# Pooled attention and a maxout FFN on one core: output stores cut by 128-token halves

## The chip, the cores and the metric

The kernel runs on one core of a Trainium2 chip. The metric is device time in microseconds. Before the change it is 230.5 us, the median of three runs (229.07 to 233.97). The profile is one more execution of the same program.

## The reference

Attention over keys and values that are averaged in groups of eight, for 8 batches of 8 heads, 576 positions and 64 dimensions a head; its output, with the heads side by side, is 4608 tokens of 512 features, and goes through an FFN whose hidden layer is the maximum of three products.

```
k_p = k.reshape(B, H, 72, 8, D).mean(axis=3);  v_p likewise
attn = softmax(q @ k_p.T / 8);  x = (attn @ v_p) -> [4608, 512]
h   = max(max(x @ w1, x @ w2), x @ w3)          # w1..w3: 512 x 768
out = h @ w_out                                 # 768 x 512, float32, [4608, 512]
```

## The kernel before

**Attention** runs batch by batch: scores on PE (tile `psf`), the exponent on ACT (`et`), the product with the values on PE (`pav`), the normalised result on DVE (`xn`). From batch 3 on the result is turned to features-by-tokens by a DMA transpose on SP's queue (`turn_x`, L256, into `xT`), and the queries of later batches likewise (L305, `qb` into `qT`). k, v and q come in by DMAs that are issued from POOL's queue and convert to 16 bits on the way.

**The FFN** takes tiles of 512 tokens, n = 0 to 8. h is w1's product plus the maximum of zero and two differences; the w1 part goes straight through a merged weight `wm`, the others through `hT`. Tiles 1 to 7 end in `out_product`: seven products per tile by a Strassen-like scheme, evacuated by ACT and DVE into an SBUF buffer `osb` of [128 partitions, 2 halves, 512 features]; a tile has two of them (j = 0 and 1), and three are in rotation. When the products of one buffer are all there, `store` writes it to DRAM. Tile 0 has its own stores in `project` (L421). Tile 8 ends in `out_last`, which runs each product for one half m of 128 tokens at a time and keeps its results in one buffer `ob`, [128, 2 (j), 2 (m), 512]; its stores are made by columns (`lo` and `hi`, 256 each) on three queues: j = 1 `hi` and j = 0 `hi` on SP, j = 1 `lo` on ACT, j = 0 `lo` on POOL.

**How tokens lie.** The kernel works on the 576 rows of a batch in nine groups of 64: group g holds the rows r * 9 + GS[g], r = 0 to 63, with GS = (0, 2, 4, 6, 8, 1, 3, 5, 7). A half m of an output buffer is two neighbouring groups: u = 0 on partitions 0 to 63 and u = 1 on 64 to 127. `store` before (L685 to L692) goes by u: the two halves m = 0 and 1 of one u are groups g and g + 2, and where GS[g + 2] = GS[g] + 4 within the batch, one DMA takes both, with the pattern 64 rows x 2 x columns in DRAM; else there are two DMAs of 64 rows each.

**Order.** The order of work on every engine is written out by hand (the string ORDER and the list for the last tile), and each queue issues in that order: on SP the stores stand between the transposes. In the built program each transfer on SP's queue also waits for the one that was issued eight transfers earlier to have landed, since eight completion semaphores are used in turn.

Of the kernel before, what the change touches and what calls it, by code (L numbers as in the profile page):

```python
# [14 lines left out]
def kernel(  # L15
# [11 lines left out]
    nc = tc.nc  # L27
# [3 lines left out]
    B, H, S, D = q.shape  # L31
# [10 lines left out]
    NG = 9  # L42
    GS = (0, 2, 4, 6, 8, 1, 3, 5, 7)
# [18 lines left out]
    def psum(shape, dtype, name, tag, bufs):  # L62
        return pools[-1].tile(shape, dtype, name=name, tag=tag, bufs=bufs)
# [5 lines left out]
    def matmul(*args, **kw):  # L69
        latest[0] = nc.tensor.matmul(*args, **kw)  # L70
        return latest[0]
# [66 lines left out]
    for sign in (1, -1):  # L138
        nc.gpsimd.affine_select(
            out=pick, in_=pick, compare_op=ALU.is_ge, fill=0.0, base=7 * (sign < 0),  # L140
            pattern=[[sign, 6], [-8 * sign, 128]], channel_multiplier=6 * sign)
    for i in range(3):
        load_w(slice(256 * i, 256 * i + 256))
    nc.gpsimd.dma_start(
        out=wo_sb, in_=moe_w_out.rearrange("(jc p) c -> p jc c", p=128))
# [378 lines left out]
    def take(key, shape=(128, 2, 256)):  # L524
        i = free_banks.pop(0)
        taken[key] = i, psum(list(shape), F32, name="pb", tag=f"pb{i}", bufs=1)
        return taken[key][1]

    def give(key):
        free_banks.append(taken.pop(key)[0])  # L530
# [80 lines left out]
    def of(i):  # L611
        return "B" if i == 2 else "C" if i in (4, 7) else "A"
# [69 lines left out]
            nc.vector.tensor_tensor(out=hTs[n][:, j, c], in0=relus[j], in1=b, op=ALU.max)  # L682
        give("n")

    def store(e, n, j, o, c):  # L685
        for u in range(2):
            b, g = divmod(2 * (4 * n + 2 * j) + u, NG)
            pair = g + 2 < NG and GS[g + 2] == GS[g] + 4
            for m in range(0, 2, 1 + pair):
                b, g = divmod(2 * (4 * n + 2 * j + m) + u, NG)  # L690
                dst = out[S * b:S * b + S, :].rearrange("(r g) c -> r g c", g=NG)
                e.dma_start(out=dst[:, GS[g]:GS[g] + 4 * pair + 1:4, c],  # L692
                            in_=o[64 * u:64 * u + 64, m:m + 1 + pair, c])

    def out_operands(n, i, m, r):
        za, zb = PRODUCTS[i]
        c = slice(128 * m, 128 * m + 128)
        if isinstance(zb, str):
            z = int(zb[1]) - 1
            left = xs[n % 2][:, z, r, c] if r < 2 else ths[n][:, z, r - 2, c]  # L700
        else:
            at = HALF * (zb % 2) + 128 * m
            left = (tokens(NB * n + at, NB * n + at + 128)[:, 2 * (zb // 2) + r] if r < 2
                    else hTs[n][:, JH * (zb // 2) + r - 2, at:at + 128])
        h, r = (0, r) if r < 2 else (1, r - 2)
        right = so[h][:, int(za[1]) - 1, r] if isinstance(za, str) else out_w(za, h)[:, r]
        return left, right

    outs = {}
    lo, hi = slice(0, HALF), slice(HALF, C)  # L710

    def out_product(n, i):
# [27 lines left out]
        if i in (5, 7, 3) and all((n, z, "d") in done for z in (5, 7, 3)):  # L740
            store(nc.sync, n, 1, o(1), slice(0, C))
        if i in (2, 4) and all((n, z, "d") in done for z in (2, 4)):
            store(nc.sync, n, 0, o(0), slice(0, C))

    def out_last(n):

        o = sb2.tile([128, 2304], F32, name="ob", tag="et")[:, 0:2048].rearrange(
            "p (j m c) -> p j m c", j=2, m=2)
        banks, ended = {}, set()

        def product(i, m):
            f = of(i)
            if (f, m) not in banks:
                banks[f, m] = (psum([128, HALF], F32, name="oC", tag=SC[0], bufs=SC[1])
                               if f == "C" else take((f, m), (128, HALF)))
            p = banks[f, m]
            for r in range(5):
                matmul(p, *out_operands(n, i, m, r), stop=(r == 4),
                                 start=(i in FIRST and r == 0), skip_group_check=True)
            ended.add((i, m))  # L760

            def plus(j, c):
                nc.vector.tensor_tensor(out=o[:, j, m, c], in0=o[:, j, m, c],  # L763
                                        in1=banks["B" if c == lo else "C", m], op=ALU.add)

            def both_of(*parts):
                return all((z, k) in ended for z in parts for k in range(2))

            if i in (1, 5, 6, 3):
                nc.scalar.copy(out=o[:, int(i in (5, 3)), m, lo if i in (1, 3) else hi],  # L770
                               in_=p)
            elif i == 2:
                plus(0, lo)
            elif i == 4:
                plus(0, hi)
            if i in (5, 7) and (12 - i, m) in ended:
                plus(1, hi)
            if i in (2, 3):
                give((f, m))
            if i in (5, 7) and both_of(5, 7):  # L780
                store(nc.sync, n, 1, o[:, 1], hi)
            if i == 3 and both_of(3):
                store(nc.scalar, n, 1, o[:, 1], lo)
            if i in (2, 4) and both_of(i):
                store((nc.gpsimd, nc.sync)[i // 4], n, 0, o[:, 0], (lo, hi)[i // 4])

        return product

# [149 lines left out]
```

## Time and profile before

| | |
|---|---|
| median of three runs | 230.5 us |
| profiled execution: time, span | 227.75 us, 225.9 us |
| mean granted clock of TensorE | 0.997 |
| L692 stores from `osb`, SP's queue | 43, issue 476 / 608 / 1189 ns (min / median / max) |
| L692 stores from `ob` | 4 on SP, 2 on POOL, 2 on ACT |
| landing of stores from `osb` after issue | 2.3 / 3.1 / 8.2 us |
| transposes on SP's queue | 27 for `xT`, 15 for `qT` |

The span is the time from the first to the last instruction in the profile; what the profiled execution took beyond it lies before and after. Landing is the time from the issue of a transfer to its completion semaphore. "SPq" and "ACTq" in the profile are the instruction streams of SP and ACT as they issue transfers.

### The profile page before, as it was taken

The page shows a single profiled execution, that of the slowest core. Times are in us where ns is not written, and L with a number is a line of the kernel's source. Part 1 is how long each engine was busy: PE and PEld are TensorE (multiplying, and loading weights), DVE is VectorE, ACT ScalarE, POOL GpSimd, SP SyncE. Part 2 cuts the span into 40 slices and gives each one's busy share as a digit, 9 for nine tenths or more (in the row PEclk, how much of TensorE's full clock was granted, in tenths as well). Part 3 has the DMA queues.
Part 4 walks back from the last instruction along what each step waited for, and adds up shares of the span by engine and source line. Part 5 has one row for each costly group of instructions (what it writes and reads, how often), then busy time and mean ns, then how long its engine had stood idle before and what let it go on. Part 6 is the DMA issues. An engine that isn't in the chain of part 4 may idle for free.

```text
span 225.9 us, 5235 instructions
## 1 busy us (share of the span) xinstructions
PE 212.3 (94%) x2046; PEld 165.7 (73%) x2046; DVE 180.2 (80%) x362; ACT 132.0 (58%) x264; POOL 82.7 (37%) x90
## 2 busy tenths in 40 slices
PE   7788999899999999998999996999999999999991
PEld 2377745558986666874679885988989898888881
DVE  3558967276999899987899965989989998988651
ACT  2267525687866887354369855957454571674230
POOL 7975300969419546459012027125140000000020
PEclk9999999999999999999999999999999999999998
DMA  6999999989999799989999999995371541430085
GB/s 166 208 197 197 204 207 205 204 160 236 151 156 132 126 163 182 151 171 194 134 211 172 155 125 171 195 156 107 70 166 36 136 105 31 115 73 0 4 229 141
DMA packets 50824, 33.57 MB, mean 149 GB/s; under 512 B 27280, under 2 KB 46352, under 8 KB 50800
## 3 DMA queue, kind: packets, MB, share of 16 engines
q0 software_dynamic: 20304, 16.98, 51.6%
q1 hardware_dynamic: 30208, 16.00, 40.8%
q8 instruction: 16, 0.26, 0.5%
q10 hardware_dynamic: 288, 0.26, 0.4%
q14 instruction: 8, 0.07, 0.1%
HBM read 34.60 MB, written 9.44 MB: 195 GB/s over the span
## 4 chain that ended last, share of the span: by engine, by line
PE 73%; DVE 11%; DMA 9%; issue 3%; ACT 1%; POOL 1%; SPq 0%; POOLq 0%; DVEq 0%; ACTq 0%
PE pb L70 54%; PE psf L70 5%; DMA qT<-qb 5%; PE pw L70 4%; PE pav L70 4%; DMA vt<-in_v_dram 4%; DVE xn L279 3%; PE pm L70 2%; PE pxt L74 1%; DVE hT L682 1%; DVE xs L537 1%; PE oC L70 1%; DVE kz L78 1%; DVE hs L537 1%; DVE rcp L277 1%
## 5 line engine op out<-in xcount | busy, mean ns | idle before, releaser
L70 PE MATMUL pb<-xT,mw 128*128 128x256 f16 (+1 forms) x312 | 52.8, 305 | 1.2 <-DVE hT L682 1.2
L70 PEld LDWEIGHTS <-mw 128*128 128x128 f16 x444 | 41.5, 98 | 16.3 <-issue 2.2
L807 POOL TENSOR_TENSOR half<-vt 72x512 f32<-72x512 f16 x28 | 32.9, 1189 | 52.9 <-DMA vt<-in_v_dram 42.6
L226 ACT ACTIVATE et<-psf 72x512 f16<-72x512 f32 x63 | 35.3, 595 | 8.2 <-PE psf L70 8.1
L279 DVE TENSOR_TENSOR xn<-pav,rcp 128x512 f16<-128x512 f32 x40 | 27.7, 691 | 1.4
L78 ACT COPY osb<-pb 128x512 f32<-128x512 f32 x25 | 14.7, 587 | 23.7 <-PE pb L70 23.7
L70 PE MATMUL psf<-qT,kz 128*128 128x256 bf16 (+4 forms) x161 | 21.3, 249 | 2.6 <-DMA qT<-qb 2.0
L636 DVE TENSOR_TENSOR ys<-ys,pb 128x512 f16<-128x512 f16 x30 | 20.3, 682 | 2.3 <-PE pb L70 2.0
L70 PEld LDWEIGHTS <-kz 128*128 128x128 bf16 x185 | 14.6, 98 | 8.5 <-issue 3.4
L70 PEld LDWEIGHTS <-hs 128*128 128x128 f16 x192 | 18.8, 98 | 2.2
L811 POOL TENSOR_TENSOR vt<-half 72x512 f16<-72x512 f32 x14 | 18.0, 1300 | 5.9 <-DVE xs L537 3.4
L692 POOL DMA_DIRECT2D out_dram<-ob x2 | 1.3, 636 | 50.1 <-DVE ob L763 50.1
L70 PE MATMUL pb<-mwo,hT 128*128 128x256 f16 (+1 forms) x120 | 19.3, 294 | 0.0
L70 PE MATMUL pb<-soh,hs 128*128 128x256 f16 x138 | 19.1, 273 | 0.0
L70 PEld LDWEIGHTS <-hT 128*128 128x128 f16 x168 | 16.3, 98 | 3.6
L78 ACT COPY pb<-pb 128x512 f32<-128x512 f32 x21 | 12.0, 575 | 10.8 <-PE pb L70 7.0
L70 PE MATMUL pav<-vp,et 72*128 72x65 f16 x320 | 17.1, 194 | 0.8 <-DVE xn L279 0.4
L78 ACT CAST ys<-pb 128x512 f16<-128x512 f32 x27 | 15.6, 593 | 3.6 <-PE pb L70 3.3
L70 PE MATMUL pb<-xs,sums 128*128 128x256 f16 x90 | 17.2, 272 | 0.1
L70 PEld LDWEIGHTS <-et 72*128 72x128 f16 x320 | 14.6, 98 | 3.5 <-DVE xn L279 1.4
L70 PE MATMUL pb<-xs,sw 128*128 128x256 f16 x90 | 17.2, 272 | 0.0
L645 ACT ACTIVATE t<-pb 128x256 f16<-128x256 f32 x30 | 11.2, 387 | 8.2 <-PE pb L70 7.8
(111 smaller groups left out, 413.0 us busy)
## 6 DMA issues: line engine op xcount, KB each, us to landing
out_dram<-osb SPq DMA_DIRECT2D x38, 128.0 KB, 2.7
ktFalse<-in_k_dram POOLq DMA_DIRECT2D x7, 576.0 KB, 13.2
qb<-in_q_dram POOLq DMA_DIRECT2D x7, 576.0 KB, 9.5
vt<-in_v_dram POOLq DMA_DIRECT2D x7, 576.0 KB, 14.1
out_dram<-osb SPq DMA_DIRECT2D x13, 256.0 KB, 3.7
mw<-in_moe_w_dram POOLq DMA_DIRECT2D x9, 256.0 KB, 9.5
ktTrue<-in_k_dram SPq DMA_DIRECT2D x3, 384.0 KB, 5.5
mwo<-in_moe_w_out_dram POOLq DMA_DIRECT2D x1, 768.0 KB, 13.3
```

What stands on the lines that cost most here:

```text
L70: latest[0] = nc.tensor.matmul(*args, **kw)
L74: latest[0] = nc.tensor.transpose(*args, **kw)
L78: (nc.vector.tensor_copy if on_vector[0] else nc.scalar.copy)(out=out, in_=in_)
L226: nc.scalar.activation(out=out, in_=in_, func=FT.Exp, scale=1.0 / 64.0)
L277: nc.vector.reciprocal(out=rcp, in_=pv[:, :, :, 64])
L279: nc.vector.tensor_tensor(out=xn, in0=pv[:, :, :, 0:D], in1=rcp.to_broadcast([128, 2, 4, D]), op=ALU.mult)
L537: t = e.tensor_tensor(out=out, in0=a, in1=b, op=op)
L636: nc.vector.tensor_tensor(out=y[:, j], in0=y[:, j], in1=bank("C", n, g), op=ALU.add)
L645: nc.scalar.activation(out=t0, in_=p[:, 0], func=FT.Relu)
L682: nc.vector.tensor_tensor(out=hTs[n][:, j, c], in0=relus[j], in1=b, op=ALU.max)
L807: yield e.tensor_tensor(out=f[:, c], in0=t[:, c, 0:4, :], in1=t[:, c, 4:8, :], op=ALU.add)
L811: yield e.tensor_tensor(out=t[:, c, 0:2, :], in0=f[:, c, 0:2, :], in1=f[:, c, 2:4, :], op=ALU.add)
```

## The change

`store` gets a list of halves, `parts`. Where both groups of a half lie two rows apart in one batch (GS[g + 1] = GS[g] + 2, that is for g other than 4 and 8) for all halves asked for, it issues one DMA per half: source the 128 partitions of that half, destination the pattern 2 groups x 64 rows x columns. Else it goes on as before. In `out_last` the last store (j = 0, `hi`) is issued for each half m as soon as that half's addition has been recorded, and no longer once for both.

```
-    def store(e, n, j, o, c):
+    def store(e, n, j, o, c, parts=(0, 1)):
+        whole = [m for m in parts if 2 * (4 * n + 2 * j + m) % NG not in (4, 8)]
+        if len(whole) == len(parts):
+            for m in parts:
+                b, g = divmod(2 * (4 * n + 2 * j + m), NG)
+                dst = out[S * b:S * b + S, :].rearrange("(r g) c -> r g c", g=NG)
+                e.dma_start(out=dst[:, GS[g]:GS[g] + 3:2, c].rearrange("r u c -> u r c"),
+                            in_=o[:, m, c])
+            return
         for u in range(2):
...
-            if i in (2, 4) and both_of(i):
-                store((nc.gpsimd, nc.sync)[i // 4], n, 0, o[:, 0], (lo, hi)[i // 4])
+            if i == 2 and both_of(2):
+                store(nc.gpsimd, n, 0, o[:, 0], lo)
+            if i == 4:
+                store(nc.sync, n, 0, o[:, 0], hi, (m,))
```

In the built programs nothing else differs on PE, ACT, DVE or POOL. SP issues 50 plain transfers in place of 58: from `osb`, 14 of 2x64x512 and 21 of the old forms in place of 43 of the old forms; from `ob`, 4 of 2x64x256 in place of 4 of 64x2x256. ACT's two stores and POOL's two have the new form 2x64x256 too. Of the transposes, those that follow the first new stores on SP's queue are the ones that the profile of before has from 101.78 us on.

## The prediction

> **What bounds the kernel now.** I read the page's slices first, then the chain that ended last, then the transfer views of single stages. The slices:
>
> ```profile
> span 225.9 us, 5235 instructions
> ...
> PE 212.3 (94%) x2046; PEld 165.7 (73%) x2046; DVE 180.2 (80%) x362; ACT 132.0 (58%) x264; POOL 82.7 (37%) x90
> ...
> DMA  6999999989999799989999999995371541430085
> ```
>
> PE is busy 94% of the span, so the kernel is PE-bound on average. But the DMA engines stand at nine tenths and over through slice 28, to about 158 us: until then whatever is put on an engine in addition comes out behind what is there. The chain between 95 and 200 us has one long piece that is no PE work:
>
> ```profile
> 126.84 0.32 SPq L256
> 127.16 0.05 issue
> 127.21 0.02 SPq L305
> 127.22 0.03 issue
> 127.25 10.34 DMA qT<-qb
> 137.59 0.04 issue
> 137.64 0.60 PE psf L70 x5
> ```
>
> A transpose by DMA, issued on SP's queue like the stores, lands at 137.59 us and PE uses it 0.05 us later. Issue and landing events give the same for its neighbours: the qT transposes issued at 103.51 and 108.13 land 2.7 and 1.6 us ahead of their first use, those issued at 143.98 and 145.37 0.9 and 1.5 us ahead. SP's queue is a just-in-time supply between 100 and 155 us. The end:
>
> ```profile
> 219.69 3.36 SPq L692 DMA_DIRECT2D out_dram<-ob  x4
> ...
> 220.66 1.37 ACTq L692 DMA_DIRECT2D out_dram<-ob  x2
> ...
> 220.81 0.97 DVE L763 TENSOR_TENSOR ob<-ob,oC 128x256 f32<-128x256 f32 x2 [1.15 <-PE oC L70]
> ```
>
> DVE's last addition ends at 221.78, two stores are issued one after the other (221.80, 222.44), and the last lands at 224.89: the tail is issue and landing, not PE.
>
> **Sum of the intended part.** SP issues 8 stores fewer (58 plain transfers become 50), at a median of 608 ns each, 4.9 us of its queue. Two come out ahead of the transposes of 101.78 us and two ahead of those of 119.27 us; PE waited for neither group, so I take nothing. At the end the store for m=0 waits for the first of the two additions alone (ends near 221.3); SP is free since 220.98, so issues stand at 221.3 and 221.95 instead of 221.80 and 222.44, and the last landing, 2.45 us after its issue, moves from 224.89 to 224.4: -0.5 us. What is late next is then the ACT store that lands at 223.99.
>
> **What it adds.** In the built programs every store of before has the 64 rows as the slowest count of its pattern in DRAM (64x512, 64x2x512, 64x2x256); the loads have 72, 96 or 128. The new ones have 2x64x512 and 2x64x256: slowest count 2. No row of before shows a transfer with a slowest count under 64, so its price has two ends. If the rows are still dealt out to 16 engines, a store costs what it did. If it is dealt out along its slowest count, two engines carry it: 64 rows each in place of 8 (of a whole 256 KB store), or 64 of 1 KB. I take the second, because the slowest count is the only count that both forms of store have in the same place.
>
> [...] No trace here shows a slowest count of 2.
>
> Price of a packet on a fed engine: the transfer views of 160 to 168, 193 to 201 and 221 to 226 us, where only stores and one transpose run.
>
> ```profile
> GB/s 218 169 13 0 0 41 0 0 0 0 0 0 215 225 174 184 184 164 143 297 236 266 277 369 379 379 307 287 184 215 256 241 207 197 218 177 78 65 35 19
> ...
> out_dram<-osb SPq DMA_DIRECT2D x4, 256.0 KB, 4.3
> ```
> ```profile
> q1 hardware_dynamic: 640, 1.05, 56.3%
> ```
> ```profile
> GB/s 164 221 197 188 189 189 213 221 156 172 213 361 369 230 180 205 246 172 205 279 287 328 262 246 270 213 180 82 8 0 0 0 0 0 0 0 0 0 0 0
> ...
> q1 hardware_dynamic: 570, 0.52, 42.4%
> ```
>
> Best slices: 379 GB/s over 16 engines is 23.7 GB/s on one, 86 ns for 2 KB; 369 is 23.1, 44 ns for 1 KB. Dearest: 56.3% of 16 engines for 8 us over 512 packets is 141 ns for 2 KB; 42.4% of 16 for 5 us over 512 packets is 66 ns for 1 KB. A queue with 64 packets waiting keeps its engine fed, so I take the low prices and keep the high ones for the range. A 256 KB store is then 64 x 86 ns = 5.5 us of both engines, 56 packets or 4.8 us more than now; behind it on the two engines stand the transposes, which need all 16.
>
> Stage by stage, by the times of before (each stall moves what follows, loads included, so they add):
> - 96.8 us, two such stores (four issues now): 9.6 us more in front of the transposes issued from 101.78; least slack 1.6 us: +7 (a little is made good by SP's two saved issues). Their buffer, whose next writer is ACT's copy at 108.50, comes free near 99.1 + 11 = 110.4, which the same stall covers.
> - 113.6 us, two: 9.6 more, slack 0.05 at 137.6: +9.6.
> - 139.6 us, two: 9.6 more, slack 0.9: +8.7.
> - 161.1 us, four, with no load beside them: 256 packets from 163.4 on, 22 us, to 185.4. The xT transposes behind them now land by 174.57; DVE's sums (queued behind which stand the hT and xn operations that PE needs) take them at 176.4: +9. ACT's copy into their buffer (169.78) waits to 174.9, inside the same 9.
> - 193.4 us, four: no transpose follows, packets end at 217.4; the first two have landed at 206.4, before ACT reuses the buffer (208.5): 0.
> - The tail: four stores on SP and two on ACT, 6 x 64 packets of 1 KB: 16.9 us from the first packet (221.85): 238.8 against 224.9: +14. POOL's two are issued 2.3 us before the first of SP's; I count nothing for them.
> Each SP transfer also waits for the landing of the one eight before it (the built program's order), which holds back transposes that would queue on the two engines anyway: 0, at most what is counted already.
>
> Sum: 7 + 9.6 + 8.7 + 9 + 14 = +48, less 0.5. The profiled execution has 225.9 of span and 227.75 in all; 225.9 + 48 + 1.85 gives 276, and the median of the three runs (230.5) lies 2.75 above the profiled one: **279 us**. With the dear prices: 15.8 more per pair gives 14 + 15.8 + 15, the four 23, the buffers at 208.5 some 5, the tail 22: +95, 325 us.
>
> **Rivals.**
> 1. *Stalls cost clock too.* Granted clock is 1.00 in every window from 95 to 219 us and 0.89 from 219 to 226, where PE works 2.32 of 7 us: idle time takes 0.8 us of full clock there. Four stalls at that: +3, 282 us. For it: the stalls of 7 to 10 us exceed that idle time. Against: the loss of that last window may be mostly after the last matmul. [...]
> 2. *Only the tail pays.* The transposes move in small packets; if they pass the stores on the two engines instead of queueing, or the engines overlap packets, the middle is hidden: +14, 244 us. For it: the xT transposes issued from 148 to 159 us have 2.7 us of slack and more. Against: the chain's piece at 127.25 with none.
> 3. *Not slower: the spread stays at 16 engines*, because the transfer is cut by its 128 rows in SBUF, or the pattern is turned around before it runs. Place: each store; it decides if the landing of one 2x64x512 store stays near 3.7 us. Then only the -0.5 us is left, or up to -1.8 with the saved issues ahead of 127.25: 229 to 230 us, no measurable difference. For it: SBUF's side still has 128 rows. Against: DRAM's has 2.
>
> **Numbers.** Forecast 0.55, the clock 0.25, the tail alone 0.12, the spread 0.08. The three runs of before differ by 2.1%, so 2% is about what can be told from no change. Slower by over 2%: the first three cases, 0.92, less 0.01 for a spread-like mixture: 0.91; within: 0.08; faster: 0.01. The range runs from the tail alone (245) to some seven tenths of the way to the dear end (312); outside are the spread, and about 0.1 of the tails of the others. The forecast's own range is 258 to 312.
>
> **What would show it.** Right: landing of 2x64 stores at 8 us and more in place of 3.6 to 4.9; PE waiting for qT and xT, DVE for xT, ACT for out_dram; two engines' worth of DMA share (about one eighth) for 17 us after the last matmul. Wrong: landings as before and a tail of 3 us (rival 3); long landings with PE still at 90% to 219 us (rival 2); a granted clock under 0.95 in the middle slices (rival 1).

## The result and the profile after

The changed kernel takes 284.97 us, median of four runs (282.38 to 288.14), against 231.67 us (229.07 to 233.97) for the kernel before beside it: a ratio of 1.236 [1.213, 1.260], slower. (Some executions come out over 1.5% slower than the fastest of their kernel; the medians are of all executions, the ratios with their 95% intervals of the others alone.) The profiled execution took 282.38 us with a span of 280.3 us, 54.4 more than the 225.9 of before.

The page of the changed kernel (busy time, slices, and queue 10, which is ACT's: packets, MB, share):

```profile
span 280.3 us, 5225 instructions
...
PE 224.9 (80%) x2046; PEld 172.4 (62%) x2046; DVE 181.8 (65%) x362; ACT 132.3 (47%) x264; POOL 82.6 (29%) x90
...
PEclk9999999999999999599977799599986899999855
DMA  7999998999999959399939493711199310116311
...
q10 hardware_dynamic: 260, 0.26, 0.3%
```

PE does the same 2046 matmuls. The 54.4 us divide without a remainder. PE is idle for 55.4 us (280.3 - 224.9) where it was idle for 13.6, which is 41.8 more: 15.9 of these lie after the last matmul (20.5 us to the end, 4.6 before) and 25.9 in the middle. The other 12.6 (224.9 - 212.3) are the same matmuls made longer by a lower granted clock. It is 0.909 on average where it was 0.997, and PEclk shows it as four groups of low digits; the fifth, at the end, lies behind the last matmul and costs nothing.

The last fenced line bears on how many engines a store runs. Before, it was:

```profile
q10 hardware_dynamic: 288, 0.26, 0.4%
```

ACT's queue carries two stores, both of the new form. Each has 128 data packets of 1 KB per 128 KB; 288 packets were 256 of data and 2 x 16 small ones, and 260 are 256 and 2 x 2. The small ones are completions: the semaphore of an old store gets 16 updates in the trace, that of a new one 2 (194.78 and 194.82 us for the first of tile 4). Read as one completion from each engine that carries a part, a new store runs on two engines and an old one on sixteen; the rate at the end, below, fits two. SP's queue has the same counts: 58 plain transfers at 16 completions are 928; 32 old at 16 and 18 new at 2 are 548; the page's count for that queue falls by 380, from 30208 to 29828.

The chain of waits of the changed kernel between 95 and 282 us (start, length, what):

```profile
97.08 18.16 DMA out_dram<-osb
...
131.00 20.43 DMA xT<-xn
...
163.76 13.45 DMA qT<-qb
...
187.38 12.56 DMA out_dram<-osb
...
201.17 5.81 PE pb L70 x37
206.98 6.18 DMA xT<-xn
```

Before, the chain of this stretch had one long transfer (10.34 us, a transpose). Now it has five, and two of them are stores. The waits, over the whole span (who, for what: us in total, times, longest):

```profile
ACT osb L78 <- DMA out_dram<-osb: 23.5, 4, 9.5
...
DVE xs L537 <- DMA xT<-xn: 11.3, 2, 5.9
...
PE psf L70 <- DMA qT<-qb: 5.9, 1, 5.9
...
PE pb L70 <- DMA xT<-xn: 2.8, 1, 2.8
```

The first did not exist before: ACT, which evacuates products for PE, stands still until an output buffer has been written out. The second was 3.4 us, the third 2.0.

SP's own queue, as it issues (start, us, instruction; 96 to 125 us of the changed kernel):

```profile
96.39 1.22 SPq L691 DMA_DIRECT2D out_dram<-osb  x2
97.71 6.43 SPq L700 DMA_DIRECT2D out_dram<-osb  x3
104.24 4.85 SPq L256 DMA_TRANSPOSE xT<-xn  x1
109.13 5.97 SPq L305 DMA_TRANSPOSE qT<-qb  x1
```

The two new stores are issued in 0.6 us each. The three old stores behind them take 6.43 us to issue and the two transposes behind those 4.85 and 5.97, where before an old store took 0.6 us and a transpose here 1.7 to 1.8. The two stores of 96.39 and 97.08 land at 104.39 and 115.23.

The end, first the timeline and then the transfers of 263 to 279 us (40 slices, and queue, packets, MB, share of 16 engines):

```profile
257.64 13.26 SPq L691 DMA_DIRECT2D out_dram<-ob  x4
...
259.28 0.97 DVE L771 TENSOR_TENSOR ob<-ob,oC 128x256 f32<-128x256 f32 x2 [1.15 <-PE oC L70]
```
```profile
GB/s 61 49 49 49 49 49 49 46 49 49 49 49 49 46 49 49 49 49 49 49 46 49 49 49 49 46 49 49 49 49 49 49 46 49 49 49 49 49 46 18
...
q1 hardware_dynamic: 526, 0.53, 9.5%
q10 hardware_dynamic: 227, 0.23, 4.1%
```

DVE's last addition ends at 260.25 and the last store lands at 279.27, 19.0 us later (3.1 before). Meanwhile 49 GB/s flow at a level rate, and the two queues keep 13.6% of 16 engines busy, or 2.2 of them. With two completions a store, that is some 24.5 GB/s on each of two engines, the same two for both queues, and fourteen idle.

### The profile page after: what moved, and what is told of

Its sections match the earlier page's. It is cut to its first block, busy times and chain, and to the rows that moved or that the text cites. A ratio compares the mean times of both kernels' runs of the same rounds, so it can differ in the third digit from the quotient of the medians.

```text
span 280.3 us, 5225 instructions
## 1 busy us (share of the span) xinstructions
PE 224.9 (80%) x2046; PEld 172.4 (62%) x2046; DVE 181.8 (65%) x362; ACT 132.3 (47%) x264; POOL 82.6 (29%) x90
## 4 chain that ended last, share of the span: by engine, by line
PE 52%; DMA 27%; DVE 8%; issue 2%; SPq 2%; ACT 1%; ACTq 0%; DVEq 0%
PE pb L70 35%; DMA out_dram<-osb 11%; DMA xT<-xn 9%; DMA qT<-qb 5%; PE psf L70 4%; PE pw L70 3%; PE pav L70 3%; DMA ktTrue<-in_k_dram 2%; PE pm L70 2%; DVE xn L279 2%; PE pxt L74 1%; DVE halfh L537 1%; SPq L700 1%; PE oC L70 1%; DVE kz L78 1%
## 5 line engine op out<-in xcount | busy, mean ns | idle before, releaser
L70 PE MATMUL pb<-xT,mw 128*128 128x256 f16 (+1 forms) x312 | 56.9, 321 | 15.6 <-ACT t L680 6.5
L70 PEld LDWEIGHTS <-mw 128*128 128x128 f16 x444 | 43.2, 102 | 33.1 <-issue 17.8
L817 POOL TENSOR_TENSOR half<-vt 72x512 f32<-72x512 f16 x28 | 32.3, 1167 | 70.3 <-DMA vt<-in_v_dram 53.7
L70 PE MATMUL psf<-qT,kz 128*128 128x256 bf16 (+4 forms) x161 | 23.3, 263 | 6.5 <-DMA qT<-qb 5.9
L70 PEld LDWEIGHTS <-kz 128*128 128x128 bf16 x185 | 15.4, 102 | 13.1 <-issue 7.5
L735 DVE TENSOR_TENSOR osb<-osb,pb 128x512 f32<-128x512 f32 x14 | 9.6, 684 | 15.2 <-ACT osb L78 11.3
L70 PEld LDWEIGHTS <-hT 128*128 128x128 f16 x168 | 16.7, 100 | 3.9
L70 PE MATMUL pb<-xs,sums 128*128 128x256 f16 x90 | 18.7, 292 | 0.0
L70 PE MATMUL pav<-vp,et 72*128 72x65 f16 x320 | 17.8, 198 | 1.0 <-DVE xn L279 0.6
L70 PE MATMUL pb<-xs,sw 128*128 128x256 f16 x90 | 18.5, 289 | 0.0
L70 PEld LDWEIGHTS <-et 72*128 72x128 f16 x320 | 15.4, 101 | 3.4 <-DVE xn L279 0.9
```

The costliest lines, as they stand in the source:

```text
L735: nc.vector.tensor_tensor(out=o(j)[:, :, hi], in0=o(j)[:, :, hi], in1=bank("C", n, "d"), op=ALU.add)
L817: yield e.tensor_tensor(out=f[:, c], in0=t[:, c, 0:4, :], in1=t[:, c, 4:8, :], op=ALU.add)
```

## The experiments

**Is it the order of the counts, and nothing else of the change?** Two forms that keep the cut by halves and give the work to more engines. In the first the pattern runs over the rows first, so the rows of the two groups come out mixed in DRAM and the output is not the reference's:

```
-                e.dma_start(out=dst[:, GS[g]:GS[g] + 3:2, c].rearrange("r u c -> u r c"),
+                e.dma_start(out=dst[:, GS[g]:GS[g] + 3:2, c],
```

> The changed kernel with every new store's DRAM pattern written 64x2 in place of 2x64: the same number of transfers, the same halves, queues, waits, bytes and rows, the slowest count 64 in place of 2. The two groups of each half come out with their rows mixed, so the output is not the reference's. Theory (a store is dealt out along its slowest count, so the changed kernel's ran on two engines): 230 to 232 us, landings of the new stores under 5 us, 16 completions a store in the packet count, mean granted clock back at 0.99, last landing about 2.5 us after the last addition. Rival (the cost is in storing by halves as such: 128-partition transfers, other places in SP's queue, other landings to wait for): 280 us and over.

Measured: 225.98 us (10 runs) against 229.73 beside it, ratio 0.994 [0.989, 1.000]. Queue 10 and the end, from the page and the timeline of this kernel:

```profile
q10 hardware_dynamic: 288, 0.26, 0.3%
```
```profile
219.67 3.65 SPq L691 DMA_DIRECT2D out_dram<-ob  x4
...
221.55 0.96 DVE L771 TENSOR_TENSOR ob<-ob,oC 128x256 f32<-128x256 f32 x2 [1.15 <-PE oC L70]
```

The stores are as many, as large and at the same places of each queue as in the changed kernel; only 2x64 became 64x2. With that the 16 completions are back and the whole loss is gone. The last landing (224.84) is 2.33 us behind DVE's last addition (222.51), where it was 3.11: the early half of the last store gains 0.8 us in these two executions. That is the part of the change that does what it was laid out for. It is too small for the median to show.

In the second form each half goes out as two transfers of 64 rows, with every row at its place:

```
-                e.dma_start(out=dst[:, GS[g]:GS[g] + 3:2, c].rearrange("r u c -> u r c"),
-                            in_=o[:, m, c])
+                for u in range(2):
+                    e.dma_start(out=dst[:, GS[g + u], c],
+                                in_=o[64 * u:64 * u + 64, m, c])
```

> The changed kernel with each half stored by two transfers of 64 rows, one for each group: the halves and the half-by-half store at the end stay, the number of transfers grows (SP issues 68 plain ones in place of 50, before 58), slowest count 64. Theory (slowest count): 231 to 234 us, the last store issued some 0.8 us later than before because four issues stand at the end in place of two. Rival (storing by halves as such): 280 us and over.

Measured: 229.77 us (two runs), ratio 1.013 [1.001, 1.024], with 320 packets on queue 10 (256 and 4 x 16). From DVE's last addition to the last landing it is 3.58 us, 0.5 more than before: what the early half gains, the extra issues take. So the cut by halves has no fault in itself, and no worth either once it needs two issues.

**How the loss divides.** The new form in the last tile alone, and in the middle tiles alone:

```
-        if len(whole) == len(parts):
+        if n == LAST and len(whole) == len(parts):
```

> Only the last tile stores in the new form; tiles 1 to 7 store as before. Theory (the parts add: the profile of the changed kernel has 15.9 us more between the last matmul and the end): 231.7 + 16 = 247 to 248 us, PE as before up to 221 us. Rival (the tail was long because the middle's stores still stood on the two engines): under 240 us.

```
-        if len(whole) == len(parts):
+        if n < LAST and len(whole) == len(parts):
...
-            if i == 2 and both_of(2):
-                store(nc.gpsimd, n, 0, o[:, 0], lo)
-            if i == 4:
-                store(nc.sync, n, 0, o[:, 0], hi, (m,))
+            if i in (2, 4) and both_of(i):
+                store((nc.gpsimd, nc.sync)[i // 4], n, 0, o[:, 0], (lo, hi)[i // 4])
```

> Only tiles 1 to 7 store in the new form; the last tile stores as before. Theory (the last matmul stood 38.5 us later in the changed kernel): 231.7 + 38.5 = 270 us, granted clock near 0.93, the tail from the last matmul on about 5 us as before. Rival (the stalls come from the last tile's changes or are shared with it): under 255 us.

Measured: the tail alone 245.14 us, 1.077 [1.069, 1.086]; the middle alone 269.15, 1.187 [1.181, 1.193]; against the same 229.73 these are +15.4 and +39.4, together 54.8. The traces say the same: held against before, the first is 15.3 us longer behind its last matmul, and the second comes to its last matmul 40.0 us later; together 55.3, where the changed kernel has 54.4. So neither hides the other by more than about 1 us. (By the ratios alone the parts come to more than the whole, 26% against 24%; the kernel before scattered by 4% in that set.) Matmuls take 212.3 us in the first, exactly as before, and 222.0 in the second: the clock cost matmul time in the middle only, where PE stops and goes on.

**The same four stores at two places.** The new form in one middle tile each, n = 4 (stored near 161 us before, with transposes behind it) and n = 6 (near 193 us, with none); the last tile as before in both:

```
-        if len(whole) == len(parts):
+        if n == 4 and len(whole) == len(parts):
```

> The kernel before with the new form for tile 4 alone: four 2x64 stores of 256 KB, issued near 161 us, with no loads beside them, transposes behind them and their buffers wanted again 8 us later. Theory (a store on two engines costs what waits for it: buffer or transposes): the ledger of matmul starts in the changed kernel gives 12.5 us for this place, so 229.7 + 12 = 241 to 243 us, PE's clock under 1.00 only after that stall. Rival (the cost is the time on the two engines, 4 x 5.1 = 20 us, wherever it is): 250 us.

> The kernel before with the new form for tile 6 alone: the same four stores issued near 193 us, where no transpose follows and the buffers are wanted 15 us later. Theory (what waits for it): 0 to +1 us, 229.7 to 231 us, although the last of the four lands about 23 us after its issue by SP's order. Rival (time on the two engines, wherever): 250 us; second rival (the stores of the last tile, issued from 213 us, come out late behind them): +3 us and more.

Measured: tile 4 costs 244.02 against 229.81 us, 1.058 [1.048, 1.068], or 14.2 us; tile 6 costs nothing, 228.96, 0.997 [0.991, 1.003]. In tile 4's trace the matmuls are 16.8 us late at the end, but 4.7 of that were lost ahead of its stores, most of it at a wait for qT near 138 us and in slower matmuls behind it; 12.0 us are the stores'. The chain of the kernel with tile 4, where its stores stand:

```profile
166.54 12.51 DMA out_dram<-osb
...
186.38 5.85 DMA xT<-xn
```

Its waits name the same two: ACT stands 5.3 us for the buffer, and DVE 11.7 us in all for xT, of which the longest is 6.1. In the changed kernel the four stores land 5.1 us apart in tile 6 as in tile 4, so they take as long; but in tile 6 nothing that PE needs waits for them.

**Which wait holds the middle?** If it were the buffer alone, a fourth buffer should free it; if the transposes behind the stores are nearly as late, it should move the wait and gain little. To make room, the warm-up tile was halved (its matmuls read 256 columns twice in place of 512 once) and `xn` has five buffers:

```
-        return sb3.tile([128, 2, C], F32, name="osb", tag="osb", bufs=3)
+        return sb3.tile([128, 2, C], F32, name="osb", tag="osb", bufs=4)
...
-        xn = sb3.tile([128, 2, 4, D], F16, name="xn", tag="xn", bufs=6)
+        xn = sb3.tile([128, 2, 4, D], F16, name="xn", tag="xn", bufs=5)
```

> The changed kernel with four output buffers in rotation in place of three; to make room the ring of normalised attention tiles has 5 in place of 6, and the warm-up matmuls at the start read 256 columns twice in place of 512 once. Theory (both waits stand nearly level: where the buffer's is taken away the transposes' comes 2 to 4 us earlier and no more): 278 to 283 us, ACT's wait for out_dram gone and PE's or DVE's for qT and xT longer. Rival (the buffers carry the middle: ACT's wait for out_dram is 23.5 us in all): 262 us or less.

Measured: 283.32 us, 1.229 [1.217, 1.240] (the changed kernel itself, in another set, had 1.235 [1.229, 1.241]). ACT's wait for the buffer is gone, and the waits of 95 to 262 us show where it went:

```profile
DVE xs L537 <- DMA xT<-xn: 30.6, 3, 14.9
...
PE psf L70 <- DMA qT<-qb: 12.7, 3, 6.5
PE pb L70 <- DMA xT<-xn: 11.9, 1, 11.9
```

(This execution took 287.3 us, 4 above the median, so the lines are read for who waits.) With the buffer free, the engines that need the transposes wait in its place. The converse takes the stores off the transposes' queue and leaves the buffers at three:

```
+                e = nc.scalar if n < LAST else e
                 e.dma_start(out=dst[:, GS[g]:GS[g] + 3:2, c].rearrange("r u c -> u r c"),
```

> The changed kernel with the 14 new stores of tiles 1 to 7 issued on ACT's queue in place of SP's, so that the transposes no longer stand behind them on the same queue, though on the same two engines. Theory (order in the queue delays the transposes): landings of xT and qT transposes back under 15 us and no wait of PE or DVE for them over 3 us, but ACT, which must now wait for each earlier landing before it issues, holds the evacuations: 265 to 290 us in all. Rival (the two engines' load alone delays the transposes, whatever the queue): their landings stay at 14 to 20 us.

Measured: 286.96 us, one run. The wait of DVE for xT is gone, PE waits 3.6 us for qT, and of ACT's waits these are the long ones that come from stores:

```profile
ACT osb L78 <- DMA out_dram<-osb: 17.8, 2, 11.4
...
ACT pb L78 <- issue: 17.4, 2, 9.0
PE pb L70 <- ACT pb L78: 16.7, 2, 9.8
```

Here both theories were half right. Where no loads run (the transposes behind tile 4), their landings fell from 13.9, 8.1 and 7.3 us to 7.3, 4.5 and 2.4; beside the loads they stayed at 14 to 18 us, so there a queue of their own did not bring them forward. The total stayed, but this does not show the buffer alone to be as long: ACT, which evacuates PE's products, now issues the stores itself, and was held at the issue as SP had been (8.4 us for the fourth store of tile 4, 4.8 for that of tile 6). PE waited 16.7 us for that and 13.9 for the buffer. What the two experiments show together is that the narrow stores hold the middle up in three places, the buffers, the transposes and the issue, and that taking away one leaves the total where it was; how long each would be alone was not measured.

**What is the lower clock worth?** The changed kernel with matmuls of no use put in front of the six longest idle places (25, 15, 8, 23, 14 and 17 of them):

```
+    FILL = {958: 25, 1166: 15, 1198: 8, 1379: 23, 1578: 14, 1640: 17}
...
+        fill = FILL.get(count[0], 0)
...
+            for _ in range(fill):
+                nc.tensor.matmul(idle[:, 0], warm[:, 0:128], warm, start=True, stop=True)
```

> The changed kernel with matmuls that nothing reads (warm-up operands, 512 columns, into the bank of the attention product) put in front of the six matmuls where PE stood idle for over 2 us in the middle: 25, 15, 8, 23, 14 and 17 of them, each batch a little shorter than its idle time. All data, stores and waits stay. Theory (12.6 us of the 53 are matmuls that run at a lower granted clock after the stalls, 224.9 us of PE busy against 212.3, and idle time is what lowers the clock): 6 to 11 us less than the changed kernel, granted clock 1.00 in the middle slices, the waits for stores and transposes as long as before or longer by what is gained. Rival (the clock falls for another reason, or what it costs is hidden in the next wait): within 3 us of the changed kernel.

> The changed kernel itself, for comparison on the same chip: 282 to 286 us.

Measured, side by side: 280.41 us, 1.223 [1.216, 1.231] with them and 283.11 us, 1.235 [1.229, 1.241] without. In the kernel with them:

```profile
PEclk9999999999999999999999899999689999999855
```
```profile
ACT osb L88 <- DMA out_dram<-osb: 26.2, 4, 9.5
```

The granted clock from 95 to 255 us is 0.97, where the changed kernel had 0.93 in the execution beside it and 0.89 in the first one. So between a half and three quarters of the loss were made good, and 2.7 us came of it (the difference of the ratios, 0.012, is hardly above their uncertainty), while the matmuls of the changed kernel took 9.8 us (222.1 of busy time in the execution beside) to 12.6 us longer than before. ACT's wait for the stores, 24.7 us in the execution beside, became 26.2.

That does not yet tell what the low clock costs, for in two of the six places the matmuls of no use outlasted the idle time. They write to the bank of the attention product, and in the fifth place that bank came free late:

```profile
PE pav L78 <- DVE xn L289: 5.5, 1, 5.5
```

ACT's copy that the next real matmul needs ended at 196.80 us; the batch began only at 198.42 and the real matmul at 203.56, 6.7 us late. In the sixth place the result of DVE that PE waits for in the changed kernel was already there at 209.46 us, and the batch held PE from 210.50 to 214.00. Held against the execution of the changed kernel beside it, the filled one was 2.1 us ahead at the first batch, 4.2 ahead where the fifth begins, 0.5 ahead after the sixth, and 2.6 ahead at the end. The last 2.1 are a clean price: in the changed kernel the matmuls after the last stop take that much longer, and PE waits for nothing long after them. So 2.7 us is what this mixture gave, and more likely too little than too much; the full price of the clock stays open, and the 6 us at the lower end of the theory are not excluded.

**Is something left to gain?** What is sound in the change is its early last issue. A try on the kernel before: the second of the last two stores on ACT's queue, so that they are issued side by side.

```
-                e.dma_start(out=dst[:, GS[g]:GS[g] + 4 * pair + 1:4, c],
+                (nc.scalar if u and n == LAST and j == 0 and c == hi else e).dma_start(
+                            out=dst[:, GS[g]:GS[g] + 4 * pair + 1:4, c],
```

> The kernel before; of the last two stores the second is issued on ACT's queue in place of SP's, so that they no longer wait for one another's issue. Theory (the tail is issue and landing): last landing 0.4 us earlier after the last addition, the time 229 us, a ratio that can't be told from 1. Rival (ACT's queue holds it back behind its own two stores): 0 to +0.5 us in the tail.

> The same kernel as last_pair_two_queues once more, with more rounds. There the ratio was 0.991 with an interval under 1, while its trace has only 0.1 us less between the last addition and the last landing. Theory (the gain is what the tail shows, the rest of that ratio is scatter): ratio 0.998 to 1.002. Rival (a real gain that the tail does not show): 0.987 to 0.995 again.

Measured: 227.21 us, 0.991 [0.986, 0.996] the first time, and 227.97, 1.000 [0.995, 1.005] over 12 runs the second. The trace of the first has 3.01 us from DVE's last addition to the last landing, 0.1 less than before, which cannot make a gain of 0.9%. The second, longer comparison stands: no difference. No version was found that measurably beats the kernel before. A last tile whose halves lie in DRAM as 64x2 at the right rows should keep the 0.8 us; it needs the tokens dealt to PE in another order, and was not tried.

## Why the prediction was right, point by point

The direction, the mechanism and the places were right; 284.97 us lies in the range of 245 to 312, and 6 above the 279. Each stage of the forecast can be held against the start of the same matmuls in both traces:

| stage (time before) | forecast, us | measured, us |
|---|---|---|
| 96.8, two new stores | 7 | 8.2 |
| 113.6, two | 9.6 | 9.6 |
| 139.6, two | 8.7 | 7.8 |
| 161.1, four | 9 | 12.8 |
| 193.4, four | 0 | 0.0 |
| after the last matmul | 13.5 (14 - 0.5) | 15.9 |
| sum (of unrounded figures) | 47.8 | 54.4 |

Of the 38.5 us up to the last matmul some 11.6 are matmuls that ran slower right after a stop; the stops themselves add up to 26.9, less than the 34.3 that the forecast had for them. That the stages came out so near is therefore in part luck: the sum had the clock at nothing and the stops too long. How long the stops would have been at full clock is not known, since slower matmuls also leave less to wait for.

- **The spread.** Two engines were taken, and 2 completions a store, with 2.2 of 16 engines busy at the end, fit two. The 64x2 form differs in the order of the counts alone and has 16 completions and no loss, so in these stores the spread went with the slowest count in DRAM. The rival of an even spread has fallen. The sum also lets all new stores share the same two engines, which no run of before shows; six stores on two queues with 2.2 engines busy show it for the tail.
- **The price.** 86 ns for 2 KB and 44 ns for 1 KB were taken from the best slices of before. In the changed kernel tile 6's four, which have the two engines nearly to themselves (49 GB/s from 234 to 251 us), land 5.13 us apart, 80 ns for each of 64 packets; the packets of the tail take 46 ns at the median. Beside loads the price was near the dear end (141): see the next point.
- **96.8 us.** The size held, the reason did not. The forecast let the transposes carry the stall and had the buffer free near 110.4; it came free at 115.23, and ACT's copy into it ends the longest wait. The 128 packets that these two stores have on each of the two engines took 17.6 us (the first at 97.62, the landing at 115.23), 138 ns each and not 86; loads and three stores of the old form were moving in the same time. The transposes of this stage were then in time by 0 to 2.5 us.
- **113.6 and 139.6 us.** As forecast, through the transposes (each has 16 completions in the trace, as an old store has; before, from 152.3 to 153.4 us, transposes alone held the DMA share at nine tenths and over): DMA xT at 131.00 and DMA qT at 163.76 stand in the chain, and PE goes on 0.13 and 0.04 us after they land. In the first of the two, PE had already stood 4.2 us for the buffer.
- **161.1 us is the stage that was sized too small.** The forecast's 9 us were one wait for xT, with ACT's wait for the buffer inside it. It came as two stops: PE goes on with the buffer at 201.17, works for 5.8 us and stops again until xT is there. Together the stops cost 4.1 + 4.8 = 8.9 us, as forecast; the other 3.9 are the matmuls after each of them, 1.7 and 2.2 us slower, which the sum had at nothing. The tile alone, without the stages ahead of it, shows the same: stops of 4.1 and 5.2, slower matmuls of 1.3 and 1.4.
- **193.4 us.** Nothing was forecast, and neither the changed kernel nor the tile alone measured anything.
- **The tail.** 16.9 us of packets were forecast. At 49 GB/s the six stores (0.79 MB) are 16.1 us, and the rest of the 19.0 is the start: SP's first packet moved at 263.02, 5.4 us after its issue. The stores that POOL issues were counted at nothing, but they took 6.4 us to land (3.6 in the 64x2 form) just ahead of the last six. That they are what delayed the start was not tested by itself. The tail alone measured 15.4 us by the medians.
- **"Only the tail pays"** (244 us) falls with the middle alone at 269.15 us. The transposes did not pass the stores: in the changed kernel the one issued at 131.00 us took 20.43 us to land, against at most 14.4 for xT before.
- **"Stalls cost clock too"** was true, and its 282 us came nearest. The trace has six stretches at half clock before the last matmul, of 3.4 or 6.8 us, one for each stop of 2.8 to 6.5 us and none for the one of 1.4. Matmuls took 12.6 us longer, 2.1 us for each. The +3 had no ground in the row that it was taken from: in the trace of before, the low clock of 219 to 226 us begins at 224.50, after the last matmul (221.32), and cost PE nothing. The stage at 161.1 and the tail, 3.8 and 2.4 us over their terms, hold most of what the sum lacked, and the 3.8 is this clock. How much of the rest of the 12.6 reaches the end is open, as said at the filled kernel.

## What to carry to other kernels

For every DMA look at the slowest count of its pattern in DRAM before looking at its bytes: here a count of 2 there saved eight issues on SP, but it took the completions of a store from 16 to 2 and the kernel from 231.67 to 284.97 us, where 64x2 lost nothing (225.98). Count the completions in the profile's packets to see what the program really does. The price of the narrow stores depended on what was behind them, from nothing to 12 or 14 us for the same four stores here, and freeing one of several waits that have the same cause (a buffer, a queue) gained next to nothing. An experiment that fills idle time has to be read in its own trace: does the filling end before the wait does?

## What was not expected of the hardware

- **The issue itself was held back.** Behind each pair of new stores from `osb`, SP took 2.9 to 4.9 us to issue one or both of the next two stores, and up to 9.6 us for a transpose, against 0.6 and 1.7 to 1.8 us before in the stretch of 96 to 105 us. The narrow stores thus held their queue already at the issue, and the transposes behind them started late, not only landed late. Where ACT issued them, it was ACT that stood, for up to 8.4 us.
- **A short stop was enough to lower the clock.** After one of 2.8 us it stood at half for 6.8 us; in the six stops the clock fell 2.1 to 4.9 us after PE had stopped.
- **One engine's rate hardly changed.** With two engines taken for a new store it was some 24.5 GB/s with 1 KB packets and 25.5 with 2 KB (64 x 2 KB in 5.13 us), with fourteen others idle; in the best slices of before, with 16 taken to be at work, it was 23.1 and 23.7.
